# Probabilities times values: one 128-column matmul per head, or two of 64 columns

## The chip, the cores and the metric

The kernel runs on one core of one Trainium2 chip. The metric is the device time of one execution in microseconds (us), median of several runs. The engines are PE (TensorE: matmuls, with its weight loads shown apart as PEld), DVE (VectorE), ACT (ScalarE), POOL (GpSimd) and SP (SyncE, which here only issues DMAs). A matmul multiplies a stationary operand, loaded into the array by a weight load, with a moving operand that streams through, and writes to a bank of PSUM.

## The reference

Local attention with block summaries, then two dense layers. For each of 2 batches and 8 heads (768 positions, 64 features), a query sees the keys less than 16 positions away, and 24 summaries (the maximum of the keys, the mean of the values, over blocks of 32):

```python
k_sum = k.reshape(B, H, nb, 32, D).max(axis=3);  v_sum = v.reshape(B, H, nb, 32, D).mean(axis=3)
scores_l = where(|i - j| < 16, scale * q @ k.T, -1e9)
scores_s = scale * q @ k_sum.T + log(32)
a = exp(concat(scores_l, scores_s) - rowmax);  a = a / (a.sum(-1) + 1e-9)
x = a @ concat(v, v_sum)                      # to (1536 tokens, 512)
xn = x / rms(x) * rms_g;  x = (silu(xn @ w_gate) * (xn @ w_val)) @ w_out
h = relu(x @ w_in);  out = (s * h * h + b) @ w_out2
```

## The kernel before

**Tiles.** The 1536 tokens are 12 tiles `i` of 128 queries (6 per batch, `t` within the batch). The 8 heads are two groups `g` of four, so that attention is 24 units `(i, g)`. A tile of 128 queries is two halves `c` of 64, and each half has keys of its own: 96 of its window and the 24 summaries, 120 (`KC`) in all. Keys and values lie ready per half: `vv[:, c, ...]` are the 120 value rows of half `c`.

**One unit.** `do_qk` (L587): four matmuls, scores of 128 queries against 120 keys each (the queries are laid out in `qz` so that each half meets its own keys). `do_top` (L597, DVE): mask and row minimum, one instruction per head. `do_exp` (L604, ACT): exponential and row sum, in `sm`. `do_t` (L615, PE): transposes the probabilities. `do_pt` (L634, ACT): copies them from PSUM to `PT`, 120 keys x 512 (four heads of 128 queries). `do_pv` (L643, PE): for each head one matmul with the 128 columns of `PT` as stationary operand and the values of *both* halves, 2 x 64 columns, as moving one; a bank `X` of 128 x 512 holds for each head 128 queries x (values of half 0, values of half 1), and for each query only the part of its own half is used. `do_rc` (POOL): the reciprocal of the row sums. `do_norm` (L652, DVE): for each half `c`, 64 queries x 4 heads x 64 features from `X`, times the reciprocal, to `xn`; so two instructions per unit.

**After both groups of a tile:** squares and their sum (L673, ACT), `rms` (L678 and L679, POOL), the scaling (L681, DVE), four transposes (L689, PE), and two copies as a high and a low part into `x` (L702 on ACT, L704 on DVE), the moving operand of the dense layers.

**Around it.** DVE also finds the maxima of keys (L292) and the sums of values (L332), and turns 64-bit weights into 32-bit ones (L218 to L220); ACT and POOL split each weight strip into a high part (L231) and a low part (L235). The means of values of batch 1 are put into their places by DMAs that SP issues (`spread_v`, L357). The dense layers' matmuls are L789, L790, L793 (`mm12`) and, in the last layer, L912, L913, L915.

**What sets the order.** `plan` lists all attention work, and the first 18 pairs of gate and value products of the first dense layer (`HEAD`), as tasks with an engine, a cost in us, dependencies, a rank, the buffers that they take and give, and a PSUM bank (at most three for `X`). `give_out` walks through a modelled time and writes out each engine's instructions, the task of lowest rank that can run, first. Each engine runs its instructions in that order. Where the modelled PE would stand still for over 0.6 us, `give_out` puts four transposes of the identity into a free bank (L459), whose result nobody reads. In the plan a PV task costs 0.88 us and one normalisation `dve(256)`, 0.337 us. After the plan, `moe` writes the rest of the dense layers as plain loops.

Of the kernel before, what the change touches and what calls it, by code (L numbers as in the profile page):

```python
# [18 lines left out]
NB, NH, SEQ, HD = 2, 8, 768, 64  # L19
# [8 lines left out]
KC = KW + NS  # L28
CH = 8
NCH, NWCH = KC // CH, KW // CH  # L30
GH = 4
# [26 lines left out]
def kernel(ctx: ExitStack, tc: tile.TileContext, q_t, k_t, v_w, v_t, w_gate, w_val, w_out, w_in2, w_out2, rms_g, s2, b2, out):  # L58
    nc = tc.nc
# [41 lines left out]
    def bank(i):  # L101
        return psp.tile([128, 512], F32, tag=f"b{i}", name=f"b{i}")
# [261 lines left out]
    def task(eng, us, fn, deps=(), rank=0.0, take=(), give=(), bank=None, free=(), more=0.09):  # L364

        t = dict(eng=eng, us=us, fn=fn, deps=[d for d in deps if d is not None], rank=rank, take=take, give=give,
                 bank=bank, free=free, more=more, end=None)
        tasks.append(t)
        return t
# [92 lines left out]
    def dve(n):  # L462
        return 0.07 + 1.042e-3 * n

    def act(n):
        return 0.13 + 0.74e-3 * n
# [7 lines left out]
    def plan(x):  # L474
# [96 lines left out]
        X_of = {}  # L571
        us = [(i, g) for g in range(2) for i in range(2)] + [(i, g) for i in range(2, NT) for g in range(2)]
        qk, pv, sm_of, rms_of, E = {}, {}, {}, {}, {}
        box = {}
        prev_qk = None
        for n, (i, g) in enumerate(us):
# [12 lines left out]
            deps = [Q[i, g], *[o for j in range(GH) for o in KM[b, GH * g + j]]]  # L589
# [36 lines left out]
            rc = task(RCENG, 1.35 if RCENG == "POOL" else 0.2, do_rc, ex, n - 1 if RCENG == "POOL" else n)  # L626
# [10 lines left out]
            def do_pv(bk, i=i, g=g, b=b, t=t):  # L637
                X = box["X", i, g] = bank(bk)
                PT = box["PT", i, g]
                vv = vst[b][2 * t // NTL][0:KC, 2 * t % NTL:2 * t % NTL + 2]  # L640
                for j in range(GH):
                    h = GH * g + j
                    nc.tensor.matmul(X[:, j * 128:(j + 1) * 128].rearrange("p (c d) -> p c d", c=2), PT[0:KC, j * 128:(j + 1) * 128],  # L643
                                     vv[:, :, h * HD:(h + 1) * HD], start=True, stop=True)
            C = pv[i, g] = task("PE", 0.88, do_pv, [pt, V[b, t], *VM[b, t, "ok"]], n + 0.2, bank="X", give=(("PT", pt),))

            def do_norm(c, i=i, g=g):
                if i not in X_of:
                    X_of[i] = xnp.tile([128, DM], F32, tag="xn", name="xn")
                p = slice(64 * c, 64 * c + 64)  # L650
                xv = box["X", i, g].rearrange("p (h c d) -> p h c d", h=GH, c=2)
                nc.vector.tensor_tensor(out=X_of[i][p, g * GH * HD:(g + 1) * GH * HD].rearrange("p (h d) -> p h d", h=GH),  # L652
                                        in0=xv[p, :, c],
                                        in1=sm_of[i][p, 1, GH * g:GH * g + GH].rearrange("p (h o) -> p h o", o=1).broadcast_to([64, GH, HD]),
                                        op=ALU.mult)
            N = [task("DVE", dve(256), lambda c=c, f=do_norm: f(c), [C, rc], n + 0.0) for c in range(2)]
            N[1]["deps"].append(N[0])
            N[1]["free"] = (C,)
            if g:
                N[0]["deps"].append(box["N", i][1])  # L660
                A["deps"].append(qk[i, 0])
            if g == 0:
                N[0]["take"] = ("xn",)
                box["N0", i] = N[0]
                box["A0", i] = A
                box["N", i] = N
                continue
            N = N + box["N", i]
            N[1]["give"] = (("sm", box["A0", i]),)

            def do_rms(i=i):
                ss = box["ss", i] = smallp.tile([128, 2], F32, tag="ss", name="ss")
# [3 lines left out]
            def do_ss(i=i):  # L676
# [5 lines left out]
                out=X_of[i], in0=X_of[i], scalar=box["ss", i][:, 1:2], in1=gbc, op0=ALU.mult, op1=ALU.mult), [S, sml], n - 1)  # L682
# [7 lines left out]
            deps = [G]  # L690
# [14 lines left out]
            h = task("ACT", act(512), lambda f=two_x: f(0), [ET], n - 1.2)  # L705
# [26 lines left out]
        for s in range(NSUB):  # L732
            for j in range(HEAD):
                rk = FR[s] + j * FS
                got = {}
                for k in range(2):
                    ps = []
                    for p in range(3):
# [4 lines left out]
                        deps = [*W[2 * j + k], *[E[i] for i in range(s * TPS, (s + 1) * TPS)], *ps[-1:], first[0]]  # L743
# [32 lines left out]
                c = task("DVE", dve(512), lambda f=do_v: f(0), [b_, got[1][2]], rr, free=(got[1][0],))  # L776
                d = task("ACT", act(512), lambda f=do_v: f(1), [c, *((*free_of[j], box.get("hi")) if s == 0 else ())], rr)
# [151 lines left out]

    x = [xs0]  # L930
    plan(x)
    give_out()
    n = 2 * HEAD + MORE
# [75 lines left out]
```

## Time and profile before

| | |
|---|---|
| time, median of 3 runs | 658.63 us (654.58 to 660.88) |
| span of the profiled execution | 658.8 us |
| PE busy | 634.1 us (96%) |
| DVE busy | 396.6 us (60%) |
| ACT busy | 269.8 us (41%) |
| POOL busy | 153.8 us (23%) |

The profiled execution's first to last instruction takes 658.8 us; the runs' median lies 0.2 us from it. Busy time is the union of an engine's instructions; a PE matmul's record reaches from its start to its modelled end and overlaps with the next one's, so that the distance from one start to the next is what a matmul costs in a row of them. Attention fills the first 125 us, with dense products in between; the rest is dense layers.

### The profile page before, as it was taken

The page shows a single profiled execution, that of the slowest core. Times are in us where ns is not written, and L with a number is a line of the kernel's source. Part 1 is how long each engine was busy: PE and PEld are TensorE (multiplying, and loading weights), DVE is VectorE, ACT ScalarE, POOL GpSimd, SP SyncE. Part 2 cuts the span into 40 slices and gives each one's busy share as a digit, 9 for nine tenths or more (in the row PEclk, how much of TensorE's full clock was granted, in tenths as well). Part 3 has the DMA queues.
Part 4 walks back from the last instruction along what each step waited for, and adds up shares of the span by engine and source line. Part 5 has one row for each costly group of instructions (what it writes and reads, how often), then busy time and mean ns, then how long its engine had stood idle before and what let it go on. Part 6 is the DMA issues. An engine that isn't in the chain of part 4 may idle for free.

```text
span 658.8 us, 8381 instructions
## 1 busy us (share of the span) xinstructions
PE 634.1 (96%) x3052; PEld 529.9 (80%) x3052; DVE 396.6 (60%) x778; ACT 269.8 (41%) x615; POOL 153.8 (23%) x187
## 2 busy tenths in 40 slices
PE   4878989999999999999999999999999999999998
PEld 3777778888888888888888888888888888888886
DVE  5769999524681455554555666881278647855632
ACT  3765878332453333311333325552455035404400
POOL 3345756340331111111111111110221022102100
PEclk9989999999999999999999999999999999999999
DMA  9989951100342111111211111122021301120022
GB/s 290 266 248 269 276 160 66 33 0 14 115 135 89 59 66 67 64 66 64 65 64 65 64 60 42 61 66 93 1 96 65 97 32 65 64 65 0 1 96 97
DMA packets 20929, 59.36 MB, mean 90 GB/s; under 512 B 2664, under 2 KB 2920, under 8 KB 20888
## 3 DMA queue, kind: packets, MB, share of 16 engines
q1 hardware_dynamic: 20888, 58.83, 28.6%
q8 instruction: 24, 0.39, 0.3%
q14 instruction: 17, 0.14, 0.1%
HBM read 54.79 MB, written 3.15 MB: 88 GB/s over the span
## 4 chain that ended last, share of the span: by engine, by line
PE 86%; DVE 5%; DMA 4%; ACT 2%; SPq 1%; issue 1%; POOL 0%; DVEq 0%; ACTq 0%; POOLq 0%
PE b L793 21%; PE b L789 21%; PE b L790 21%; PE b L913 7%; PE b L915 7%; PE b L912 7%; DMA qz<-in_q_t_dram 3%; PE b L587 1%; ACT P L604 1%; SPq L357 1%; DMA hg<-in_k_t_dram 1%; PE b L643 1%; DVE ks L292 1%; DVE xn L652 1%; DVE wa L219 1%
## 5 line engine op out<-in xcount | busy, mean ns | idle before, releaser
L235 POOL TENSOR_TENSOR wl<-wa,wh 128x512 fp32r<-128x512 f32 x68 | 89.5, 1323 | 388.2 <-ACT wh L231 315.0
L789 PE MATMUL b<-x,wh 128*128 128x512 f32 x288 | 113.5, 394 | 0.3
L790 PE MATMUL b<-x,wl 128*128 128x512 f32 x288 | 112.3, 390 | 0.4 <-POOL wl L235 0.4
L231 ACT ACTIVATE wh<-wa 128x512 fp32r<-128x512 f32 x68 | 41.5, 626 | 98.8 <-PE b L915 45.5
L793 PE MATMUL b<-x,wh 128*128 128x512 f32 x288 | 77.6, 391 | 0.0
L913 PE MATMUL b<-wl,hg 128*128 128x512 f32 (+1 forms) x196 | 75.1, 385 | 0.0
L912 PE MATMUL b<-wh,hg 128*128 128x512 f32 (+1 forms) x196 | 75.1, 385 | 0.0
L789 PE MATMUL b<-y,wh 128*128 128x512 f32 x192 | 74.7, 389 | 0.0
L790 PE MATMUL b<-y,wl 128*128 128x512 f32 x192 | 74.7, 389 | 0.0
L894 DVE SCALAR_TENSOR_TENSOR b<-u,sbc 128x512 f32<-128x512 f32 x48 | 50.7, 1056 | 35.6 <-ACT u L893 35.6
L790 PEld LDWEIGHTS b<-x,wl 128*128 128x128 f32 x288 | 54.1, 188 | 11.4 <-POOL wl L235 0.7
L789 PEld LDWEIGHTS b<-x,wh 128*128 128x128 f32 x288 | 54.2, 188 | 11.3 <-issue 0.7
L793 PEld LDWEIGHTS b<-x,wh 128*128 128x128 f32 x288 | 53.6, 188 | 10.8
L789 PE MATMUL b<-hg,wh 128*128 128x512 f32 x144 | 56.0, 389 | 0.0
L790 PE MATMUL b<-hg,wl 128*128 128x512 f32 x144 | 56.0, 389 | 0.0
L814 DVE SCALAR_TENSOR_TENSOR hg<-b,bbc,hg 128x512 fp32r<-128x512 f32 x48 | 36.0, 749 | 28.2 <-ACT hg L813 28.2
L220 DVE SCALAR_TENSOR_TENSOR wa<-raw,wa 128x512 int32<-128x512 int32 x68 | 50.5, 743 | 2.1
L915 PE MATMUL b<-wh,hg 128*128 128x512 f32 (+1 forms) x196 | 51.5, 385 | 0.0
L793 PE MATMUL b<-y,wh 128*128 128x512 f32 x192 | 51.3, 389 | 0.0
L219 DVE SCALAR_TENSOR_TENSOR wa<-raw,wa 128x512 int32<-128x512 int32 x68 | 49.9, 734 | 2.1
L813 ACT ACTIVATE hg<-b,bbc 128x512 fp32r<-128x512 f32 x48 | 33.0, 687 | 42.9 <-DVE b L894 42.9
L921 DVE TENSOR_TENSOR part<-b,part 128x512 f32<-128x512 f32 (+1 forms) x37 | 24.4, 673 | 43.4 <-PE b L915 43.4
(94 smaller groups left out, 1010.3 us busy)
## 6 DMA issues: line engine op xcount, KB each, us to landing
raw<-in_w_out_dram SPq DMA_DIRECT2D x28, 512.0 KB
raw<-in_w_in_dram SPq DMA_DIRECT2D x16, 512.0 KB
qz<-in_q_t_dram SPq DMA_DIRECT2D x24, 256.0 KB
raw<-in_w_gate_dram SPq DMA_DIRECT2D x12, 512.0 KB
raw<-in_w_val_dram SPq DMA_DIRECT2D x12, 512.0 KB
vt<-in_v_t_dram SPq DMA_DIRECT2D x8, 384.0 KB
hg<-in_k_t_dram SPq DMA_DIRECT2D x5, 576.0 KB
out_dram<-part SPq DMA_DIRECT2D x11, 256.0 KB
```

The source lines that it names most:

```text
L219: lambda: nc.vector.scalar_tensor_tensor(out=ai, in0=hi, scalar=-0x80000000, in1=ai, op0=ALU.bitwise_and, op1=ALU.bitwise_or),
L220: lambda: nc.vector.scalar_tensor_tensor(out=ai, in0=lo, scalar=29, in1=ai, op0=ALU.logical_shift_right, op1=ALU.bitwise_or),
L231: nc.scalar.activation(out=r(h), in_=a_t[i], func=AF.Copy)
L235: nc.gpsimd.tensor_tensor(out=r(lo), in0=a_t.pop(i), in1=high[i], op=ALU.subtract)
L789: nc.tensor.matmul(ps, r(hi[:, kk * 128:(kk + 1) * 128]), xh, start=kk == 0, stop=False)
L790: nc.tensor.matmul(ps, r(lo[:, kk * 128:(kk + 1) * 128]), xh, start=False, stop=False)
L793: nc.tensor.matmul(ps, r(hi[:, kk * 128:(kk + 1) * 128]), r(act(kk, 1)), start=False, stop=kk == 3)
L814: nc.vector.scalar_tensor_tensor(out=r(dst[1]), in0=ps, scalar=bias, in1=dst[0], op0=ALU.add, op1=ALU.subtract)
L894: after(0, lambda u=u, ps=ps: nc.vector.scalar_tensor_tensor(out=ps, in0=u, scalar=sbc[:, 0:1], in1=u, op0=ALU.mult, op1=ALU.mult))
L912: nc.tensor.matmul(acc, gh, r(ws[e][0][:, cs]), start=e == 0, stop=False)
L913: nc.tensor.matmul(acc, gh, r(ws[e][1][:, cs]), start=False, stop=False)
L915: nc.tensor.matmul(acc, r(ge[e][:, 1]), r(ws[e][0][:, cs]), start=False, stop=e == 3)
```

## The change

Per head, `do_pv` makes two matmuls: the 64 columns of `PT` of half `c` are the stationary operand, the 64 value columns of the same half are the moving one, and the result goes to PSUM partitions 64c to 64c + 63, columns 64j to 64j + 63 of `X`. The products of a half with the other half's values are no longer made. `X` holds 128 x 256 values in use, and `do_norm` is one instruction over 128 partitions. The plan's PV task keeps its cost of 0.88; there is one normalisation task per unit in place of two.

```diff
                 for j in range(GH):
                     h = GH * g + j
-                    nc.tensor.matmul(X[:, j * 128:(j + 1) * 128].rearrange("p (c d) -> p c d", c=2), PT[0:KC, j * 128:(j + 1) * 128],
-                                     vv[:, :, h * HD:(h + 1) * HD], start=True, stop=True)
+                    for c in range(2):
+                        nc.tensor.matmul(X[64 * c:64 * c + 64, j * HD:(j + 1) * HD], PT[0:KC, j * 128 + 64 * c:j * 128 + 64 * c + 64],
+                                         vv[:, c, h * HD:(h + 1) * HD], start=True, stop=True)
...
-            def do_norm(c, i=i, g=g):
+            def do_norm(i=i, g=g):
...
-                p = slice(64 * c, 64 * c + 64)
-                xv = box["X", i, g].rearrange("p (h c d) -> p h c d", h=GH, c=2)
-                nc.vector.tensor_tensor(out=X_of[i][p, g * GH * HD:(g + 1) * GH * HD].rearrange("p (h d) -> p h d", h=GH),
-                                        in0=xv[p, :, c],
-                                        in1=sm_of[i][p, 1, GH * g:GH * g + GH].rearrange("p (h o) -> p h o", o=1).broadcast_to([64, GH, HD]),
+                nc.vector.tensor_tensor(out=X_of[i][:, g * GH * HD:(g + 1) * GH * HD].rearrange("p (h d) -> p h d", h=GH),
+                                        in0=box["X", i, g][:, 0:GH * HD].rearrange("p (h d) -> p h d", h=GH),
+                                        in1=sm_of[i][:, 1, GH * g:GH * g + GH].rearrange("p (h o) -> p h o", o=1).broadcast_to([128, GH, HD]),
                                         op=ALU.mult)
-            N = [task("DVE", dve(256), lambda c=c, f=do_norm: f(c), [C, rc], n + 0.0) for c in range(2)]
-            N[1]["deps"].append(N[0])
-            N[1]["free"] = (C,)
+            N = [task("DVE", dve(256), do_norm, [C, rc], n + 0.0, free=(C,))]
```

## Rows read from the trace of the kernel before

**Rows 1.** Busy time by stretch: us; each engine's busy us and instructions; clock, DMA.
```profile
0.00:40.00 40.00, 26.16 (x163) 22.60 (x164) 22.90 (x98) 21.11 (x81) 14.52 (x46) 0.96 0.90 250
40.00:83.00 43.00, 39.08 (x277) 33.82 (x276) 40.36 (x137) 33.41 (x120) 27.18 (x41) 1.00 0.96 286
83.00:98.00 15.00, 12.16 (x95) 10.84 (x93) 13.72 (x37) 11.56 (x34) 9.06 (x11) 1.00 0.54 165
98.00:125.00 27.00, 26.16 (x170) 22.95 (x171) 24.46 (x73) 19.38 (x66) 14.54 (x22) 1.00 0.19 63
125.00:658.70 533.70, 530.49 (x2352) 439.72 (x2350) 295.13 (x437) 184.32 (x317) 88.45 (x68) 1.00 0.19 62
```

**Rows 2.** Chain that ended last, shares by line within 40 to 98 us.
```profile
by line: ACT P L604 12.1%; SPq L357 10.7%; issue 7.8%; DVE wa L219 6.5%; DVE ks L292 6.1%; DVE vs L332 6.0%; DVE xn L652 5.9%; DMA raw<-in_w_val_dram 5.8%; DVE P L597 5.7%; DVE wa L220 4.4%; ACT x L702 3.6%; DVE xn L681 3.5%; DVE wa L218 2.
```

**Rows 3.** The same chain in order of time (start, us, what), around two places.
```profile
15.43 9.68 DMA qz<-in_q_t_dram
25.17 10.46 DMA qz<-in_q_t_dram
...
47.78 0.42 DVE xn L652
48.20 0.60 DVE wa L220
48.83 0.34 DVE xn L652
...
85.43 0.71 SPq L357
...
92.00 3.35 DMA raw<-in_w_val_dram
95.48 0.53 issue
96.01 0.72 ACT junk L673 x2
```

**Rows 4.** Chain that ended last, shares by line from 98 us to the end.
```profile
by line: PE b L793 24.6%; PE b L789 24.5%; PE b L790 24.5%; PE b L913 7.8%; PE b L915 7.8%; PE b L912 7.8%; PE b L643 1.0%; PE b L587 0.5%; PE b L689 0.4%; PE b L615 0.4%; ACT P L604 0.2%; ACT PT L634 0.1%; DVE part L921 0.1%; DVE xn L652 0
```

**Rows 5.** Line L652 by stretch: us; DVE busy us and instructions; clock, DMA.
```profile
0.00:40.00 40.00, 3.38 (x8) 0.96 0.90 250
40.00:83.00 43.00, 6.68 (x16) 1.00 0.96 286
83.00:98.00 15.00, 4.20 (x10) 1.00 0.54 165
98.00:125.00 27.00, 5.87 (x14) 1.00 0.19 63
```

**Rows 6.** DVE groups by form, 40 to 125 us: form, count, busy us, mean ns, idle.
```profile
L652 DVE TENSOR_TENSOR xn<-b,sm 64x256 f32<-64x256 f32 x40 | 16.8, 419 | 0.7
L704 DVE TENSOR_TENSOR x<-b,x 128x512 fp32r<-128x512 f32 x12 | 8.2, 686 | 1.8 <-ACT x L702 1.7
L352 DVE TENSOR_SCALAR part<-b 24x256 f32<-24x256 f32 x2 | 0.8, 424 | 0.6 <-ACT part L354 0.6
```

**Rows 7.** Line L643 by stretch: us; PE and PEld busy us and records; clock, DMA.
```profile
40.00:83.00 43.00, 8.83 (x64) 7.84 (x64) 1.00 0.96 286
83.00:98.00 15.00, 5.96 (x48) 5.66 (x48) 1.00 0.54 165
98.00:125.00 27.00, 6.28 (x48) 5.98 (x48) 1.00 0.19 63
```

**Rows 8.** Timeline of PE, 100 to 104 us: start, us, instructions merged.
```profile
100.85 1.06 PE L643 MATMUL b<-part,PT 120*128 120x128 f32 x8
101.74 1.05 PE L587 MATMUL b<-hg,qz 128*128 128x120 f32 x8
102.63 0.60 PE L615 MATMUL b<-ident,P 128*120 128x128 f32 x4
103.07 1.05 PE L587 MATMUL b<-hg,qz 128*128 128x120 f32 x8
```

**Rows 9.** Line L643: records, duration ns min/median/max, first and last start.
```profile
L643 PEld LDWEIGHTS b<-hg,PT x96: 186/192/242, 24.4 to 70.6; 120*128 120x128 f32 x96
L643 PE MATMUL b<-hg,PT x96: 272/275/377, 24.5 to 70.7; 120*128 120x128 f32 x96
```

**Rows 10.** Timeline of PE near the end: the same product at 512 and 256 columns.
```profile
650.65 0.39 PE L912 MATMUL b<-wh,hg 128*128 128x512 f32 x1
650.88 0.39 PE L913 MATMUL b<-wl,hg 128*128 128x512 f32 x1
...
652.58 0.28 PE L913 MATMUL b<-wl,hg 128*128 128x256 f32 x1
652.70 0.28 PE L912 MATMUL b<-wh,hg 128*128 128x256 f32 x1
```

**Rows 11.** Issues by SP and an ACT row, 83 to 96 us: start, us [idle before].
```profile
83.80 8.09 SPq L357 DMA_DIRECT2D part<-part  x10
92.00 0.45 SPq L203 DMA_DIRECT2D raw<-in_w_val_dram  x1
...
95.44 0.68 ACT L209 ACTIVATE wa<-raw 128x512 f32<-128x512 f32 x1 [2.01 <-DMA raw<-in_w_val_dram]
```

More of the change, by code (lines that the diff above doesn't have):

```diff
@@ L642, in do_pv @@
                     h = GH * g + j
-                    nc.tensor.matmul(X[:, j * 128:(j + 1) * 128].rearrange("p (c d) -> p c d", c=2), PT[0:KC, j * 128:(j + 1) * 128],
-                                     vv[:, :, h * HD:(h + 1) * HD], start=True, stop=True)
+                    for c in range(2):
+                        nc.tensor.matmul(X[64 * c:64 * c + 64, j * HD:(j + 1) * HD], PT[0:KC, j * 128 + 64 * c:j * 128 + 64 * c + 64],
+                                         vv[:, c, h * HD:(h + 1) * HD], start=True, stop=True)
             C = pv[i, g] = task("PE", 0.88, do_pv, [pt, V[b, t], *VM[b, t, "ok"]], n + 0.2, bank="X", give=(("PT", pt),))
-            def do_norm(c, i=i, g=g):
+            def do_norm(i=i, g=g):
                 if i not in X_of:
                     X_of[i] = xnp.tile([128, DM], F32, tag="xn", name="xn")
-                p = slice(64 * c, 64 * c + 64)
-                xv = box["X", i, g].rearrange("p (h c d) -> p h c d", h=GH, c=2)
-                nc.vector.tensor_tensor(out=X_of[i][p, g * GH * HD:(g + 1) * GH * HD].rearrange("p (h d) -> p h d", h=GH),
-                                        in0=xv[p, :, c],
-                                        in1=sm_of[i][p, 1, GH * g:GH * g + GH].rearrange("p (h o) -> p h o", o=1).broadcast_to([64, GH, HD]),
+                nc.vector.tensor_tensor(out=X_of[i][:, g * GH * HD:(g + 1) * GH * HD].rearrange("p (h d) -> p h d", h=GH),
+                                        in0=box["X", i, g][:, 0:GH * HD].rearrange("p (h d) -> p h d", h=GH),
+                                        in1=sm_of[i][:, 1, GH * g:GH * g + GH].rearrange("p (h o) -> p h o", o=1).broadcast_to([128, GH, HD]),
                                         op=ALU.mult)
-            N = [task("DVE", dve(256), lambda c=c, f=do_norm: f(c), [C, rc], n + 0.0) for c in range(2)]
-            N[1]["deps"].append(N[0])
-            N[1]["free"] = (C,)
+            N = [task("DVE", dve(256), do_norm, [C, rc], n + 0.0, free=(C,))]
             if g:
-                N[0]["deps"].append(box["N", i][1])
+                N[0]["deps"].append(box["N", i][0])
                 A["deps"].append(qk[i, 0])
@@ L668, in plan @@
             N = N + box["N", i]
-            N[1]["give"] = (("sm", box["A0", i]),)
+            N[0]["give"] = (("sm", box["A0", i]),)
             def do_rms(i=i):
```

## The prediction

> **What bounds the kernel now.** I read the busy time by stretch first, since a share over the whole span mixes stages with different limits. From 125 us on PE is busy 530.5 of 533.7 us: that part is a fixed amount of PE work, which the change does not touch [rows 1]. So the question is when PE gets through what lies before it, attention and the dense products woven into it. There the stretches differ.
>
> Up to 40 us the chain that ended last goes through two loads of queries of 9.7 and 10.5 us [rows 3], and DVE is busy 22.9 of 40 us [rows 1]. Neither a cheaper normalisation nor a dearer matmul is seen there; I count that stretch at nothing. From 40 to 98 us DVE is busy 40.4 + 13.7 = 54.1 of 58 us, PE 39.1 + 12.2 = 51.2, so PE stands idle for 6.8 us [rows 1]. The chain there runs through many small steps of DVE and ACT, and the normalisation L652 has 5.9% of it, 3.4 us [rows 2]. From 98 us on the chain is matmuls, one after another, to the end [rows 4], and PE is busy 26.2 of the 27 us up to 125 [rows 1]. So the kernel waits for DVE (and what hangs on it) between 40 and 98, and for PE after that. The two halves of the change fall on just these two: it takes from DVE and may put on PE.
>
> **The normalisation.** Of 48 instructions 24 are left. A new one reads 128 partitions x 256 where the old one read 64 x 256 at 419 ns. No row has the new form, but a 24 x 256 read from PSUM takes 424 ns and a 128 x 512 one 686 [rows 6]: partitions do not show in the price, columns do, (686 - 419) / 256 = 1.04 ns each. I take 0.42 us for the new one, so that each unit saves 0.42 us of DVE. (If it cost twice as much for twice the partitions, nothing would be saved; the 24-partition row excludes that.) From 40 to 98 us lie 26 of the old ones, after 98 another 14 [rows 5]: 13 x 0.419 = 5.4 us and 7 x 0.419 = 2.9 us saved.
>
> What of the 5.4 us is seen? At most all of it, as DVE is 93% busy there. At least what lies on the chain: half of its 3.4 us of L652, 1.7 us. The pair at 47.78 and 48.83 shows what is removed: a second instruction of the same unit, with a weight instruction between the two [rows 3]. Against the full amount speaks the later part of this stretch: from 85 to 92 us the chain is SP issuing ten small DMAs that spread the means of values, and then a weight load, for which ACT stands still for 2.0 us [rows 3, 11]. Those 10 us get no shorter by a faster DVE; they only start earlier. I take the middle, 3.6 us. After 98 the 2.9 us are hidden under PE; PE's idle time there, 0.8 us, is all that could be won, and I count none.
>
> **The matmuls.** In the trace one unit is 8 pairs of weight load and matmul for four heads (each f32 product is two), from 100.85 to 101.74 us: 0.89 us, 111 ns a pair [rows 8]. After the change there are 16 pairs, each with 64 columns loaded and 64 streamed in place of 128 and 128. Two ends bound them. If time goes with columns, a pair takes 56 ns and the unit 0.89 as before. For that speaks the one product that the trace has at two widths: 512 columns take 0.23 us from start to start and 256 take 0.12 [rows 10]. If each pair has a floor at what it costs now, the unit takes 16 x 0.111 = 1.78 us, 0.89 more. The other pairs here, transposes and scores, take 0.11 us too ((103.07 - 102.63) / 4, [rows 8]), so nothing excludes that floor; but the product at two widths is the row nearest to what changes, and it goes with columns. To it I add the change of shape: the array would be used in halves for one unit and whole before and after. The units' neighbours in the trace follow each other without a gap [rows 8], but all of them use (nearly) all columns. If the array has to empty once, that is what a matmul takes beyond its share in a row, 275 - 111 = 0.16 us [rows 9, 8]. I take 0.89 + 0.16 = 1.05 us, and keep 0.89 and 1.78 as ends.
>
> The Trainium skill, TensorEngine Tiling (Array Packing), Key Properties, has a rule that speaks against the change: going from one tiling mode to another drains the array. The trace has no such switch, so it neither agrees nor differs; by one drain per switch and two switches per unit the term would be 0.33 us per unit in place of 0.16, and the sum 2 us higher. The Trainium skill, TensorE: Matmul & The Clock Gate, section "Wait — 56ns, not 53.3ns?", gives some 62 ns of sequencer time per matmul where the hardware does not decode it; as an estimate from that page alone the unit would be 16 x 62 = 0.99 us, between my ends.
>
> Where does it count? After 98 us every bit of PE: 6 units (48 records, [rows 7]) x 0.16 = 1.0 us. Between 40 and 98 us there are 14 units (112 records, [rows 7]), 2.2 us; PE has 6.8 us of idle time there, of which 3.6 go with the shorter stretch and 3.2 stay as cover. Idle time does not lie where the units do, so I count half, 1.1 us.
>
> **What else moves.** No DMA is added or moved by the diff itself. The normalisation waits for the matmuls and the reciprocal as before; behind it on DVE wait the row minima of the next units, for which ACT's exponentials wait, but one wait takes the place of two. The bank X comes free one DVE instruction earlier. All this counts as nothing beyond the above. The plan, though, is made anew: it gets 24 x 0.337 = 8.1 us less of DVE work, so the order on all five queues can change; that is a rival below.
>
> **Sum**, against the profiled execution's own 658.8 us: -3.6 + 1.0 + 1.1 = -1.5, 657.3 us. The median of the runs, 658.63, is 0.2 us away from that execution, so I leave it at 657.3.
>
> **Rivals.**
>
> *DVE's saving comes through in full, and the two halves run side by side.* The halves use different columns of the array and write different partitions. If both streams of a head run at once, a unit takes 8 x 56 ns = 0.45 us, 0.44 less. After 98 us that gives 6 x 0.44 = 2.6 us; before, DVE sets the pace and it gives nothing, but all of DVE's 5.4 us are seen. 658.8 - 5.4 - 2.6 = 650.8 us; without the overlap but with the 0.8 us of idle PE, 652.6. For it: DVE at 93% [rows 1]. Against it: the chain through SP and the weight load [rows 3, 11]. The Trainium skill, TensorEngine Tiling (Array Packing), Key Properties, states that different tiles can load and multiply in parallel, which is this overlap; no row here shows two matmuls of one array at once. Chance 0.2.
>
> *A short pair has a floor (the other side).* Place: the 16 pairs of a unit, above all the six units after 98 us, where nothing covers them. At the full 1.78 us: 6 x 0.89 = 5.3 us after 98, and 14 x 0.89 - 3.2 = 9.3 us before, less the 3.6 us: 658.8 + 11.0 = 669.8 us. The point from which it decides: with x us more per unit, half covered before 98, the cost is 13x; it eats the 3.6 us at x = 0.28, a unit of 1.17 us or a pair of 73 ns. For over 1% slower, 20x - 3.2 - 3.6 = 6.6, x = 0.67, a pair of 97 ns. For it: no shorter pair in the trace. Against it: the product at two widths [rows 10]. Chance 0.22, most of it between 662 and 670.
>
> *The new order.* The plan puts a load or a wait elsewhere. The price is seen in what such a place costs now: ten DMA issues of 8.1 us before a weight load, and 2.0 us of ACT idle for it [rows 11]. One such hold more or less in the stretch before 98 is 3 to 8 us in either direction: 651 or 666. Nothing in the profile tells the sign. Chance 0.1.
>
> **How the numbers follow.** About 1% (6.6 us) is what a measurement of this kernel can tell from no change, so the border is 652 and 665.2. The likeliest case (0.48) is my sum, between 653 and 663. The first rival has 0.2, mostly just below 652; the floor 0.22, of which some 0.16 lies above 665; the new order 0.1, split. Faster 0.24, same 0.54, slower 0.22. The time is 657.3; the range 650 to 667 takes in the full saving, and the floor up to a unit of some 1.6 us, and leaves the rest out.
>
> **What would show it.** Right: L652 24 times at about 0.42 us; the start-to-start of L643's pairs at 56 to 66 ns; PE's idle time between 40 and 98 some 3 us shorter; PE without gaps after that. The first rival: pairs that start two at a time, or a unit under 0.6 us. The floor: pairs at 97 ns or more. The new order: L357's ten issues, or ACT's wait for a weight, at another place than 84 to 95 us. My prediction is wrong if DVE is not what PE waited for between 40 and 98 (its busy share falls and PE's idle time stays), or if a unit's time is far from 1.05 us.

## The result

The changed kernel takes 650.91 us (median of 10 runs, 647.93 to 651.81), the kernel before 656.23 us (median of 10, 653.45 to 660.88). The ratio is 0.9899, 95% interval 0.9876 to 0.9921 (the quotient of the two medians, 0.992, lies at its upper end): 5.3 us by the medians, 6.6 us or 1.0% by the ratio, where I had forecast 1.5 us. The three runs of before that the forecast rested on (658.63) lay 2.4 us above its later median. And the profiled execution of before was a slow one: for the changed kernel, device time less span is 650.19 - 648.4 = 1.8 us, so a span of 658.8 us belongs to a time near the slowest, 660.88. (That the median lay 0.2 us from that execution compared a time with a span.) The 10.4 us between the two profiled spans are therefore more than the change is worth; the ratios carry the argument below. For the same reason the rows of single executions that follow show where time goes, and not what the change is worth.

Busy time by stretch of the kernel after, to be read beside [rows 1]:

```profile
0.00:40.00 40.00, 26.92 (x237) 22.28 (x238) 22.99 (x104) 23.39 (x88) 14.54 (x47) 0.96 0.93 267
40.00:83.00 43.00, 37.64 (x344) 31.35 (x343) 40.34 (x138) 37.21 (x132) 32.74 (x47) 1.00 0.92 277
83.00:98.00 15.00, 14.54 (x185) 12.13 (x184) 12.29 (x58) 14.44 (x58) 13.01 (x18) 1.00 0.47 156
98.00:125.00 27.00, 27.00 (x168) 21.80 (x167) 15.04 (x25) 11.96 (x28) 8.58 (x12) 1.00 0.17 59
```

DVE is as busy as before up to 83 us, but it has more done by 98 us: from there on it executes only 25 instructions before 125, where it had 73. PE is full from 83 us on (14.5 of 15, then 27 of 27), where it had 2.8 us of idle time between 83 and 98.

The normalisation (line L651 now): count, ns min/median/max, form; to [rows 6].

```profile
L651 DVE TENSOR_TENSOR xn<-b,sm x24: 408/416/425, 25.9 to 106.3; 128x256 f32<-128x256 f32 x24
```

The matmuls (L644 now): records and their ns, then the timeline of PE around two units; to [rows 8, 9].

```profile
L644 PE MATMUL b<-part,PT x192: 221/222/272, 76.5 to 106.0; 120*64 120x64 f32 x192
```

```profile
85.03 0.69 PE L644 MATMUL b<-part,PT 120*64 120x64 f32 x16
85.65 0.65 PE L615 MATMUL b<-ident,P 128*120 128x128 f32 x4
86.27 0.69 PE L644 MATMUL b<-part,PT 120*64 120x64 f32 x16
86.88 1.15 PE L587 MATMUL b<-hg,qz 128*128 128x120 f32 x8
```

Sixteen records of 222 ns fit into 0.69 us. They start in eight pairs, one record of each half (a head has two pairs, as each f32 product is two records): the two of a pair start 5 to 8 ns apart, and the next pair 58 ns after them (107 ns behind a unit's first pair). So two matmuls run in one array. The array empties behind a unit: the row that follows starts 85.65 - 85.03 = 0.62 us after the unit's start, 0.15 us after the last of the 16 starts, and its four transposes take 0.65 us in place of 0.60. Ahead of the next unit lie 86.27 - 85.65 - 4 x 0.11 = 0.18 us more, of which these rows don't tell how much is a wait for the probabilities. Other units of the same trace do: where a transpose stands ahead of a unit, the shortest distance from its start to the unit's is 0.20 us (four times), where before it was 0.11; behind a product of 512 columns it is 0.32 in place of 0.23. So the switch costs some 0.09 us ahead of a unit. With what the rows behind it are longer by (transposes 0.65 in place of 0.60, scores 1.15 in place of 1.05) a unit costs PE about 0.62 + 0.09 + 0.05 to 0.10 = 0.76 to 0.81 us, against 0.89 before.

### The profile page after: what moved, and what is told of

It reads as the page before. It is cut to its first block, busy times and chain, and to the rows that moved or that the text cites. A ratio compares the mean times of both kernels' runs of the same rounds, so it can differ in the third digit from the quotient of the medians.

```text
span 648.4 us, 8708 instructions
## 1 busy us (share of the span) xinstructions
PE 626.2 (97%) x3232; PEld 518.9 (80%) x3232; DVE 383.0 (59%) x754; ACT 269.0 (41%) x615; POOL 155.4 (24%) x187
## 4 chain that ended last, share of the span: by engine, by line
PE 88%; ACT 4%; DVE 3%; DMA 2%; POOL 1%; issue 1%; SPq 0%; DVEq 0%
PE b L786 21%; PE b L790 21%; PE b L787 21%; PE b L910 7%; PE b L912 7%; PE b L909 7%; ACT P L604 2%; PE b L587 2%; DMA qz<-in_q_t_dram 1%; DMA hg<-in_k_t_dram 1%; PE b L644 1%; ACT PT L634 1%; PE b L615 1%; DVE xn L678 0%; PE b L686 0%
## 5 line engine op out<-in xcount | busy, mean ns | idle before, releaser
L786 PEld LDWEIGHTS b<-x,wh 128*128 128x128 f32 x288 | 54.1, 188 | 11.2 <-ACT x L699 0.2
```

The source lines that it names most:

```text
L786: nc.tensor.matmul(ps, r(hi[:, kk * 128:(kk + 1) * 128]), xh, start=kk == 0, stop=False)
```

## The experiments

The change has three parts that can be had apart: the matmuls (whole columns or halves), the normalisations (two per unit or one), and the order in which the plan writes the instructions out, which follows from the number of normalisation tasks. Theory DVE: the 24 instructions that DVE no longer executes bring the gain. Rival PE: the matmuls do. Rival order: the plan's new order does.

**The halved matmuls alone**, order and normalisations of before:

```diff
-  ...matmul(X[:, j*128:(j+1)*128] ..., PT[0:KC, j*128:(j+1)*128], vv[:, :, h*HD:(h+1)*HD] ...)
+  for c in range(2): ...matmul(X[64*c:64*c+64, j*HD:(j+1)*HD], PT[0:KC, j*128+64*c:...], vv[:, c, ...] ...)
-  in0=xv[p, :, c]                 # two normalisations stay
+  in0=xv[p]                       # xv: the 256 columns now in use
```

> The 64-column matmuls alone: two normalisations per unit as before (64 partitions each, now from the 256 columns of X), and every engine's instructions in the order of the kernel before. Theory DVE (the 24 instructions that DVE no longer executes bring the 5.3 us of the medians): no gain, ratio 1.00, about 656 us. Rival PE (the halves side by side shorten a unit on PE, or let what follows start earlier): ratio 0.99, about 651 us. Rival order (the plan, which counts 8.1 us less of DVE work, writes a better order): 1.00, about 656 us. In the trace a unit should still be 8 double starts some 58 ns apart, with an empty array before and behind it.

Measured: 656.59 us, ratio 1.0013 (0.9994 to 1.0032). The matmuls alone bring nothing; the interval leaves room for a cost of up to 2 us.

**Both changes in the old order.** The plan keeps two normalisation tasks, the first issues nothing:

```diff
+                if c == 0:
+                    return
```

> The whole change to the instructions (64-column matmuls, one normalisation per unit), but the plan still counts two normalisation tasks, of which the first issues nothing, so that the order is that of the kernel before. Theory DVE: 0.99, about 651 us. Rival PE: 0.99, about 651 us. Rival order: 1.00, about 656 us.

Measured: 655.67 us, 0.9996 (0.9976 to 1.0017). With DVE's saving in hand nothing is gained: theory DVE falls as it stood, and so does PE. (In half of this kernel's executions TensorE's granted clock was lower than in almost any of the kernel before; what that hides is told below.)

**The new order alone**, with the instructions of before:

```diff
-            N = [task("DVE", dve(256), do_norm, [C, rc], n + 0.0, free=(C,))]
+            N = [task("DVE", dve(256), lambda f=do_norm: (f(0), f(1)), [C, rc], n + 0.0, free=(C,))]
```

> The instructions of the kernel before (128-column matmuls, two normalisations per unit) in the order of the changed kernel: the plan counts one normalisation task, which issues both. Theory DVE: no gain, 656 us or some us more, as DVE gets more work than its plan counts. Rival PE: 656 us. Rival order: 0.99, about 651 us.

Measured: 655.31 us, 0.9995 (0.9979 to 1.0012). The order alone falls too.

**One normalisation in the new order, with the old matmuls**:

```diff
-  in0=box["X", i, g][:, 0:GH * HD]...
+  in0=box["X", i, g].rearrange("p (h c d) -> p h c d", h=GH, c=2)[:, :, 0]
```

> 128-column matmuls as before, one normalisation over 128 partitions per unit, in the order of the changed kernel. Left out: the second half's queries are normalised from the columns of the first half's values, so half of the attention output is not what the reference computes; the work of every engine is that of the changed kernel except for PE's matmuls. Theory DVE: 0.99, about 651 us. Rival PE: 656 us. Rival order: 0.99, about 651 us.

Measured: 651.16 us, 0.9924 (0.9901 to 0.9947). And its counterpart, **the halved matmuls in the new order with two normalisations**:

> The 64-column matmuls in the order of the changed kernel, but with two normalisations of 64 partitions per unit. Theory DVE and order together: without DVE's saving the new order is worth nothing, 655 to 656 us. Rival (matmuls and order together): 651 us.

Measured: 656.72 us, 1.0012 (0.9991 to 1.0033). So the gain needs one normalisation *and* the new order; either alone gives nothing. With the halved matmuls all four cases were run: two normalisations 1.0013 in the old order and 1.0012 in the new, one normalisation 0.9996 in the old and 0.9899 in the new. What the matmuls add, 0.25% between 0.9924 and 0.9899, is not shown: the intervals overlap.

Why does the new order alone give nothing? Busy time from 36 to 98 us (columns as in [rows 1]) of the new order with the old instructions, and of the changed kernel:

```profile
36.00:98.00 62.00, 55.32 (x403) 49.74 (x401) 58.10 (x200) 50.72 (x180) 41.90 (x61) 0.97 0.79 245
```

```profile
36.00:98.00 62.00, 56.18 (x583) 47.24 (x583) 56.39 (x213) 55.17 (x202) 46.71 (x65) 1.00 0.80 247
```

DVE is busy 58.1 of 62 us for 200 instructions, and 56.4 for 213. That with two normalisations DVE is full, and so cannot use the new order, fits these rows, but no run shows it by itself. And why does the old order give nothing with one? The same row of both changes in the old order:

```profile
36.00:98.00 62.00, 53.17 (x500) 43.63 (x495) 51.78 (x164) 47.60 (x167) 36.60 (x57) 0.97 0.84 245
```

DVE now stands idle for 10.2 of 62 us. The saving is there, but as waiting. What DVE waited for (us in total, times, longest one), the four largest:

```profile
DVE xn L682 <- POOL ss L680: 3.5, 3, 1.7
DVE x L705 <- ACT x L703: 2.3, 4, 1.2
DVE ks L292 <- DMA hg<-in_k_t_dram: 1.3, 1, 1.3
DVE vs L332 <- DMA vt<-in_v_t_dram: 1.3, 1, 1.3
```

Loads are 2.6 us of this; the other waits are for POOL's `rms` and for ACT. The chain of that kernel from 34 to 112 us, shares and some of its pieces (start, us, what):

```profile
by line: DMA vt<-in_v_t_dram 22.8%; DMA hg<-in_k_t_dram 10.4%; issue 6.0%; DVE xn L682 5.5%; ACT P L604 4.5%; DVE wa L220 3.1%; DVE wa L219 3.1%; POOL sm L622 3.0%; ACT PT L634 2.8%; PE b L794 2.6%; PE b L587 2.5%; DVE vs L332 2.4%; DVE xn 
65.38 0.53 DVE wa L219
65.91 9.93 DMA vt<-in_v_t_dram
75.86 0.96 DVE vs L332
```

A third of this chain is loads: the last load of batch 1's transposed values is issued at 65.91 and lands 9.9 us later, behind other loads, and the means of values, and with them all units of batch 1, need it. (DVE has other work meanwhile: it stands still for this load for 1.3 us only.) SP's issues show what the two orders do with it. In the old order (both changes), then in the new one, each without the loads of queries (L487) in between:

```profile
53.61 0.89 SPq L282 DMA_DIRECT2D part<-in_v_w_dram  x2
59.77 0.80 SPq L282 DMA_DIRECT2D part<-in_v_w_dram  x2
64.42 0.33 SPq L282 DMA_DIRECT2D part<-in_v_w_dram  x1
65.91 0.33 SPq L327 DMA_DIRECT2D vt<-in_v_t_dram  x1
```

```profile
58.50 0.45 SPq L282 DMA_DIRECT2D part<-in_v_w_dram  x1
62.26 0.35 SPq L327 DMA_DIRECT2D vt<-in_v_t_dram  x1
64.82 0.35 SPq L203 DMA_DIRECT2D raw<-in_w_gate_dram  x1
65.21 0.43 SPq L282 DMA_DIRECT2D part<-in_v_w_dram  x1
```

Theory loads: the place of this load is what the old order lacks. **Three loads of values put behind it, in the old order with both changes:**

```diff
+        if b == 1 and s0 >= 6 and not done:
+            held.append((s0, n))          # issued right after the last load of transposed values
+            return
```

> The run before it with both changes in the old order, where only SP's order is changed: the last three loads of values of batch 1 (384 KB each) go behind the last load of transposed values. Theory loads (in the old order a faster DVE only reaches the loads sooner; 9.9 us of the chain are the wait for that last load, and three loads ahead of it are 1.18 MB, some 4 us at the 276 GB/s of that stretch): 3 to 5 us faster than before, 651 to 653 us. Rival (many small places of the order, none of them alone): no change, 655 to 656 us.

Measured: 654.58 us, 0.9966 (0.9950 to 0.9981): 2.2 us by the ratio, less than the 3 to 5 expected, but clear. **The same edit in the kernel before:**

> The kernel before with the same edit of SP's order and nothing else. Theory loads, with DVE as the bound of the kernel before: the load lands sooner, but DVE has no time for it; no change or up to 1 us, 655 to 656 us. If the place of that load alone is what the new order is worth: 651 to 653 us.

Measured: 656.19 us, 0.9998 (0.9983 to 1.0013): with two normalisations there is nothing to win, as expected. **The other way round, that load put back in the changed kernel:**

```diff
         # in load_v, behind this load of values:
+        if b == 1 and s0 == 8:
+            load_vt(b, 3, False)          # issued here, not in its own place
```

> The changed kernel, with the last load of transposed values of batch 1 put behind the next load of a weight (512 KB), of queries and of values (384 KB) in SP's order. Theory loads: 2 to 4 us of the gain are lost, 653 to 655 us. Rival: 651 us.

Measured: 652.19 us, 0.9926 (0.9903 to 0.9949), 0.27% slower than the changed kernel, where 2 to 4 us were expected; its interval overlaps the changed kernel's, so the cost isn't shown. DVE's waits of that kernel from 36 to 98 us show that it does wait for the load there (us in total, times, longest), as the changed kernel's does not:

```profile
DVE vs L336 <- DMA vt<-in_v_t_dram: 3.9, 1, 3.9
```

The load is a part, as its run in the old order shows, and not the whole. The second difference of the orders is three weight strips: in the old order (both changes) ACT starts them at 83.6, 90.2 and 93.8 us, among batch 1's units; in the changed kernel at 101.0, 101.5 and 102.1 us. **Put off until the last unit's probabilities are copied:**

```diff
+        def put_off(u, f):                # for the strips from the seventh on
+            return f if u < 2 * HEAD else lambda: rest.append(f) if not gone else f()
...
+                if (i, g) == (NT - 1, 1): # in do_pt: now issue them
```

> Both changes in the old order, with one edit: what ACT, DVE and POOL do for the last three weight strips of the plan (three ACT and POOL rows and about 6.8 us of DVE, in the old order between 78 and 100 us) is put off until the last unit's probabilities are copied, where the new order has it. Theory weights (the new order is worth something because DVE and ACT are no longer held by those strips while batch 1's units wait): 3 to 5 us faster than before, 651 to 653 us. Rival (the gain of the order is the place of the loads): 655 to 656 us.

Measured: 659.70 us, 1.0042 (1.0023 to 1.0062). With the load's place as well:

> The same, and SP's order changed as in the run that put the last load of transposed values ahead of three loads of values. If the loads and the three strips are the whole of what the new order is worth, this equals the changed kernel: 650 to 651 us, ratio 0.990. If the two overlap: 652 us. If neither matters beyond the 1.5 us of the loads: 654 to 655 us.

Measured: 658.16 us, 1.0040 (1.0017 to 1.0063). In the kernel before:

> The kernel before, with the three weight strips put off as in the other two runs and nothing else: neither the matmuls nor the normalisation changed. Theory weights, with DVE as the bound of the kernel before: 6.8 us of DVE leave the stretch that DVE sets, more than the 5.4 us of normalisations: 652 to 654 us. If the order alone is worth nothing while DVE still has both normalisations, as the run of the new order alone showed: 655 to 656 us.

Measured: 662.36 us, 1.0089 (1.0056 to 1.0122). All three are slower, where a gain was expected. That was my placing. Busy time of the first of them, and the row of PE's timeline with the gap:

```profile
98.00:125.00 27.00, 22.12 (x174) 17.76 (x173) 15.40 (x33) 13.95 (x43) 9.71 (x15) 0.94 0.18 59
113.84 1.11 PE L694 MATMUL b<-ident,xn 128*128 128x128 f32 x4 [4.88 <-DVE xn L686]
```

PE stands idle for 4.9 of 27 us: the strips now stood on DVE in front of the last tiles' scalings, and PE's transposes of those tiles stand ahead of its dense products. Behind the gap the granted clock fell, 0.94 in this row. So these runs don't tell what the strips cost in their old place. **Put off further, until the last tile's low part is copied**, so that nothing of attention is behind them:

> Both changes in the old order; the ACT, DVE and POOL work on the last three weight strips is put off until the last tile's low part is copied, so that no instruction of attention stands behind it. Theory weights: batch 1's units end 2 to 3 us sooner, as in the run that put it off less far (last unit at 107.2 us in place of 109.8), and PE has no new gap: 652 to 653 us. Rival (the strips only move): 655 to 656 us.

Measured: 653.11 us, 0.9956 (0.9937 to 0.9974). With the load's place as well:

> The same, with the last load of transposed values ahead of three loads of values. If the place of that load and of the strips is most of what the new order is worth: 650 to 652 us. If not: 653 to 655 us.

Measured: 651.87 us, 0.9936 (0.9911 to 0.9961). In the kernel before:

> The kernel before with the strips put off in the same way, nothing else changed. Theory weights, with DVE as the bound of the kernel before: 2 to 4 us faster, 652 to 654 us. If DVE's work there is not what PE waits for: 655 to 656 us.

Measured: 655.34 us, 0.9984 (0.9965 to 1.0004). Nothing that can be seen, where 2 to 4 us were expected if DVE sets the pace there. But the run doesn't test that: the expectations put 6.8 us of DVE's work for the strips between 78 and 100 us, and the trace of the kernel before has it later. ACT's rows come early; of DVE's nine rows for these strips the first stands ahead of 98 us and the others behind, where PE sets the pace, the last at 115.68:

```profile
95.31 0.42 DVE L218 TENSOR_SCALAR wa<-wa 128x512 int32<-128x512 int32 x1
100.57 0.69 DVE L219 SCALAR_TENSOR_TENSOR wa<-raw,wa 128x512 int32<-128x512 int32 x1
```

(In the old order with both changes the nine rows start between 89.25 and 108.76 us, three of them, 1.8 us, ahead of 98.) So two edits to the old order, neither by itself worth anything measurable in the kernel before, together give 0.64% (0.39 to 0.89) with both changes: about two thirds of the whole gain. The two together were not tried in the kernel before. What the last third of the new order is, these runs leave open.

**The granted clock, by execution.** Each execution has a mean granted clock of TensorE, and on record the kernels differ in it. Executions with a mean of 0.996 or more, and with less; their number, and their median in us:

| kernel | 0.996 or more | less |
|---|---|---|
| before, all rounds | 103: 656.1 | 1: 660.5 |
| new order alone | 12: 655.3 | none |
| halved matmuls, old order | 7: 655.7 | 5: 658.5 |
| halved matmuls, new order | 3: 655.8 | 9: 656.7 |
| both changes, old order | 6: 654.4 | 6: 657.7 |
| both changes, old order, load moved and strips put off further | 6: 651.6 | 1: 654.4 |
| one normalisation, new order | 5: 651.1 | 1: 653.3 |
| changed kernel | 6: 650.4 | 4: 651.4 |

The fall of the clock goes with the halved matmuls, and with longer executions. At the higher clock both changes in the old order are some 2 us faster than the kernel before: "nothing" is a gain of that size and a lower clock in half of the executions. The order's part is left all the same, 4 us between 654.4 and 650.4. This is no experiment: a gap of PE, as the one of 4.9 us above, lengthens an execution by itself and is followed by the lower clock, and no run holds the clock fixed.

**PE's price.** The same 16 matmuls with all first halves ahead of all second halves:

```diff
-  for j in range(GH):
-      for c in range(2):
+  for c in range(2):
+      for j in range(GH):
```

> The changed kernel with the order of the 8 matmuls of a unit changed: all heads' first halves, then all heads' second halves, so that neighbours use the same columns of the array. If matmuls run side by side only where neighbours use different columns, a unit takes 16 starts 58 ns apart in place of 8 double ones, 0.46 us more. PE sets the end for the last units: with 6 to 10 of 24 units uncovered 654 to 656 us. If PE has cover for all of them: 651 us.

Measured: 650.30 us, 0.9898 (0.9879 to 0.9917), the same as the changed kernel, though a unit does take longer. The chain of the changed kernel, then of this one:

```profile
92.75 0.62 PE b L644 x16
100.77 0.62 PE b L644 x16
```

```profile
92.40 0.90 PE b L644 x16
97.59 0.90 PE b L644 x16
```

0.28 us more per unit, some 6 us over 24, do not show in the time, though the two intervals would leave room for some 2 us. That PE has cover for them is argued, and not shown: in this run too these units stand on PE's own chain, with 27.0% of it between 80 and 110 us. (It is 0.28 and not the 0.46 expected because the second halves begin while the first still run: the whole unit's last matmul starts 0.74 us after its first, where sixteen starts 58 ns apart would take 0.87.)

**A better one?** The changed kernel with the load still further ahead:

> The changed kernel with SP's order changed further: three of the four loads of values of batch 1 that stand ahead of the last load of transposed values go behind it. Theory loads: putting it back cost 1.7 us, so putting it forward by 1.18 MB, some 4 us, gives up to 1 to 2 us more: 649 to 650 us. If that load is no longer waited for in the changed kernel: 651 us.

Measured: 649.74 us, 0.9900 (0.9869 to 0.9931). No different from the changed kernel: its DVE no longer waits for that load.

## Why the prediction was wrong

**What the miss is made of.** Between the medians the change is worth -5.3 us in place of -1.5. Of these 3.8 us, 1.4 are the normalisation with its order (one normalisation in the new order gave -5.0, 0.9924 of 656, in place of -3.6), and 2.4 are the matmuls (the -0.3 that is left, which can't be told from nothing, in place of +2.1).

**Where PE and DVE wait: right for the kernel before as far as its rows go, wrong as a rule for what a saving gives.** I wrote that the kernel waits for DVE between 40 and 98 us, and that the prediction is wrong if DVE's busy share falls and PE's idle time stays. In the old order with both changes just this happened:

```profile
40.00:98.00 58.00, 49.70 (x450) 40.65 (x451) 48.48 (x151) 43.60 (x154) 34.28 (x53) 0.97 0.83 241
```

DVE's busy time falls from 54.1 to 48.5 us, the saving that I had counted, and PE's idle time is 8.3 us where it was 6.8. DVE was busy almost throughout, but other waits stood right behind it. What takes DVE's place is shown only in part: 2.6 of its 10.2 us of idle time from 36 us on are waits for loads.

**The normalisation's price: right.** 24 instructions of 416 ns in place of 48 of 419.

**What of DVE's 5.4 us is seen: the step that failed in mechanism.** I took the middle of 1.7 and 5.4 us, 3.6, as if it were a property of the stretch, and put everything else that moves at nothing. How much is seen belongs to the order: in the old order nothing (0.9996; some 2 us at the higher clock), in the new one nearly all of it (5.0 us). My bound from below, half of the normalisation's time on the chain, was no bound: the chain shows what was last *this* time, and waits for loads, for POOL and for ACT stood right behind it. [rows 1] had DMA busy 0.96 of the time from 40 to 83 us, in the column that I did not use.

**The matmuls' price: the term that was mis-sized most.** I took 1.05 us a unit, 0.16 more than before, and charged 2.1 us. A unit takes 0.62 us to the next row's start and 0.14 to 0.19 for the rest of the two switches, some 0.1 less than the 0.89 of before: on PE the overlap pays for the switches, and yet the halved matmuls alone give nothing. With one normalisation in the new order they cost nothing either, 0.9924 without and 0.9899 with them. The halves run side by side, as in my first rival and as the Trainium skill has it (TensorEngine Tiling (Array Packing), Key Properties): different tiles work in parallel, and a change of mode drains the array. The trace agrees with both: starts 5 to 8 ns apart, and 0.15 us from the last half to the next whole matmul. The 62 ns of sequencer time per matmul that the Trainium skill gives with hardware decode off (TensorE: Matmul & The Clock Gate, section "Wait — 56ns, not 53.3ns?") do not bind here: two matmuls start in every 58 ns. I counted the last units as bare because PE's chain ran through them [rows 4]; the run with the halves in turn adds some 6 us to the units and no time that can be seen, so that charge was too high as well. Where PE makes up for them stays open.

**The first rival: near in time, in part by luck.** Its 650.8 us lie 0.1 us from the measured time. Its overlap is there, and DVE's 5.4 us are seen nearly in full, but only with the new order, which it did not count. The 2.6 us that it took from shorter units after 98 us are shown by no run, and it started from a span 2.6 us above the later median; the two cancel.

**The rival of the new order: right in mechanism, too small in chance.** I gave it 0.1 and no sign. A plan that gets 8.1 us less of DVE work writes another order for all five queues, and without that nothing that can be seen would have been gained. That the sign could have been read from the trace isn't shown; that DMA was nearly full in the stretch was there to be read.

**The baseline.** I put the sum on a span of 658.8 us and left it there, 2.6 us above the median of ten runs. Of the 6.4 us between 657.3 and 650.9 that is 2.6; the other 3.8 are the change.

## What to carry to other kernels

Work taken off the bounding engine is worth what the next waits leave of it: before crediting a saving, find what stands next in line at that place (here, among others, a load behind three others, and weight conversion among the units) and ask whether the order moves with it. Where a planner writes the order, a cheaper instruction and the plan that knows of it are two changes, and each may be worth nothing alone. When an edit that should help is slower, look at what stands behind the moved work in its new place.

## What the runs showed of the hardware

Two f32 matmuls with 64 stationary columns each, in different halves of the array, start 5 to 8 ns apart and keep a pace of one pair per 58 ns, where a matmul on all columns took 111 ns. Going back to all columns takes 0.15 us from the last start to the next; going to halves takes 0.09 us more than the pace before.

A DVE multiplication read from PSUM costs the same for 128 partitions as for 64: 416 ns for 128x256, 419 for 64x256.

In the profiled execution of both changes in the old order, TensorE's granted clock fell to the lower of its two levels, 1.2 GHz, after a gap of PE. Stretch, us, PE busy, PEld busy, DVE, ACT and POOL, granted clock, DMA:

```profile
80.00:82.00 2.00, 0.95 (x7) 0.63 (x6) 1.97 (x4) 1.98 (x7) 0.83 (x1) 1.00 0.33 77
82.00:84.00 2.00, 1.37 (x23) 1.25 (x25) 1.79 (x4) 2.00 (x6) 1.69 (x3) 0.75 0.26 60
84.00:86.00 2.00, 2.00 (x22) 1.88 (x19) 1.97 (x2) 1.83 (x5) 1.92 (x3) 0.50 0.32 74
86.00:88.00 2.00, 2.00 (x39) 1.82 (x38) 1.87 (x5) 1.12 (x3) 1.86 (x3) 0.90 0.34 84
```

PE had been busy 0.95 us of the 2 before. The changed kernel keeps 1.00 from 40 us on in its profiled execution; in 4 of its 10 executions the mean was lower than there. What the lower level costs a product is seen behind the gap of 4.88 us in the run with the strips put off, at 0.50 (first row) and then at 1.00:

```profile
114.00:116.00 2.00, 2.00 (x7) 1.74 (x8) 1.43 (x4) 1.01 (x2) 0.00 (x0) 0.50 0.81 246
115.18 0.63 PE L798 MATMUL b<-x,wl 128*128 128x512 f32 x1
115.61 0.63 PE L797 MATMUL b<-x,wh 128*128 128x512 f32 x1
117.94 0.39 PE L798 MATMUL b<-x,wl 128*128 128x512 f32 x1
118.17 0.39 PE L797 MATMUL b<-x,wh 128*128 128x512 f32 x1
```

A product of this form starts 0.43 us after the one before it at the lower level, and 0.23 us after it at the higher one. What the clock cost the old order as a whole was not tried by itself.
